# Opening of a sliding-window attention plus token/channel mixer kernel: loads, casts and score order of batch 0 rearranged

## The chip, the core and the metric

The kernel runs on one core of a Trainium2 chip. The core has five instruction streams that run on their own and meet through semaphores: TensorE (PE, matmuls; PEld is its weight load), VectorE (DVE), ScalarE (ACT), GpSimd (POOL) and SyncE (SP). Transfers between memory and the core run on 16 DMA engines; SP, ACT and POOL issue them. A transfer issued by POOL goes to the software queue (q0 in the profile), one issued by SP to q1, one issued by ACT to q10. The metric is the device time of one launch in microseconds (us), median over several runs.

## What is computed

For each of 8 batches: attention with 8 heads over 576 positions of 64 numbers, and then a mixer over positions and channels.

```python
scores = (1 / sqrt(64)) * q @ k.T                     # [8, 8, 576, 576]
rel = pos[:, None] - pos[None, :]
mask_plain = (rel >= 0) & (rel < 32)                  # heads 0 to 3
mask_dil = (rel >= 0) & (rel < 128) & (rel % 4 == 0)  # heads 4 to 7
attn = softmax(where(mask, scores, -1e9))
x = (attn @ v) with heads side by side                # [8, 576, 512]
h = relu(x.T @ w_tok1) @ w_tok2                       # mixes positions, 576 -> 256 -> 576
u = x + h.T
out = u + relu(u @ w_ch1) @ w_ch2                     # mixes channels, 512 -> 1536 -> 512
```

Inputs and the output are float32; matmuls run on float16 copies.

## The kernel before, in words

**Tiling.** A head has 576 positions: 512 "natural" ones and a tail of 64. Heads go in pairs, hp = 0 to 3; hp 0 and 1 have the plain window, hp 2 and 3 the dilated one. For the dilated heads only positions with the same remainder by 4 see each other, so the loads put positions m*4+r at partition m, column block r.

**Stages of a batch.** q and k are loaded in float32 (`load_qk`, tails of 64 by `load_tail`), cast to float16 (`cast_qk`, `cast_tails_qk`), turned by TensorE (`transposes`; tails of batch 0 by `first_tails`), and copied out of PSUM into `qz` and `kt`. `scores_plain` and `scores_dil` are generators of three steps for a pair of heads: one for each head's main blocks (tiles `sc`), and one for the small rest, the last block and the tail keys (tile `sm`). Each step ends with ScalarE's exponentials into `attp`, `attd` and `attt`. In batches 0 and 1 the mask is put into PSUM by a matmul of the identity with `veil`, a tile made once from the constants. `values` multiplies a head by v (tile `av`); VectorE divides by the row sum into `xn`. Then the token mixer (`h1p`, `up`), transposes of u, and the channel mixer: 12 blocks `gp` with the weight w3 (channel weight `moe_w_ch1`, three tiles of 512 columns, loaded by `load_w3` with a cast from float32) and the outputs `yp` with w4.

**Order.** All streams are scheduled by hand: the order in which the code is written is the order on each engine. For batch 0 the opening is written out line by line (lines 837 to 971). From line 973 on, later batches are interleaved with the channel mixer of the batch before, by `interleave`, which sorts steps by written times.

**The opening.** The constants (identity, permutation, masks; 128 x 672 float16) come by a transfer that POOL issues first (line 840). `emit_fixed` fills fixed tiles with zeros or ones. SP loads q and ACT loads k: heads 0 and 1, heads 2 and 3, tails, heads 4 to 7. SP then loads v in eight transfers (`load_v`): four blocks `l_vn` for the plain heads, the tail `l_vt`, two halves `l_vd` for the dilated heads, and `l_vx`. Each of these eight waits until one of the eight loads ahead of it has landed, since eight semaphores are used in turn. `warm(9)` is nine matmuls on a zero tile `idle`, with nothing that uses their results; `warm(3)` stands between the first transposes and the first scores. `ts` is the list of batch 0's score steps: `ts[5*hp]` and `ts[5*hp+1]` turn q and k of a pair (`tp(hp)` does both), and `ts[5*hp+2]` to `ts[5*hp+4]` are its three score steps (`sc(hp)` does all). POOL casts most of q, k and v, and issues the weights' transfers between these casts; a transfer that POOL issues takes time on POOL itself. Heads 4 to 7 of `values` need the casts of both `l_vd` halves and of `l_vx` (into `vt`, `cast_vx`).

**Batch 1's loads.** They are held back by `gate`: POOL writes one element into batch 1's tail tile after the copies `w2p`, and SP's loads wait for that.

Of the kernel before, what the change touches and what calls it, by code (L numbers as in the profile page):

```python
# [16 lines left out]
S = 576  # L17
# [51 lines left out]
def kernel(  # L69
# [11 lines left out]
    nc = tc.nc  # L81
# [77 lines left out]
    def emit_fixed():  # L159
        nc.gpsimd.memset(idle, 0.0)  # L160
# [7 lines left out]
        nc.vector.memset(attt, 1.0)  # L168

    def emit_fixed_late():  # L170
        for i in range(2):
            nc.gpsimd.memset(vv[i][64:128, 4], 0.0)
            nc.gpsimd.memset(vv[i][:, :, :, 64:65], 1.0)
            nc.gpsimd.memset(vt[i][:, :, 64:65], 1.0)
            nc.gpsimd.memset(w1t[i], 0.0)
        nc.gpsimd.memset(w2a[:, :, S:640], 0.0)


    l32 = {}
# [657 lines left out]
    ctx.enter_context(tc.manual_schedule())  # L837


    nc.gpsimd.dma_start(out=const, in_=const_dram)  # L840
    emit_fixed()
    new_qk(0)
    load_qk(0, "q", 0, 2, nc.sync)
    load_qk(0, "k", 0, 2, nc.scalar)
    load_qk(0, "q", 2, 4, nc.sync)
    load_qk(0, "k", 2, 4, nc.scalar)
    load_tail(0, "q", nc.sync)
    load_tail(0, "k", nc.scalar)
    load_qk(0, "q", 4, 8, nc.sync)
    load_qk(0, "k", 4, 8, nc.scalar)  # L850
    spark = fixed("spark", [1, 1], FP32)
    nc.scalar.activation(out=spark, in_=idle[0:1, 0:1], func=AF.Exp)
    load_v(0)
# [5 lines left out]
        c = slice(512 * i, 512 * i + 512)  # L859
        nc.gpsimd.dma_start(out=w3[i], in_=moe_w_ch1[:, c].rearrange("(x p) c -> p x c", p=128))  # L860

    cast_qk(0, "q", 0, nc.scalar)
    cast_qk(0, "k", 0, nc.vector)
    nc.vector.tensor_scalar(out=veil, in0=const[:, 256:CW], scalar1=1.0, scalar2=60000.0,
                            op0=ALU.subtract, op1=ALU.mult)
    cast_qk(0, "q", 1, nc.gpsimd)
    emit_fixed_late()
    cast_tails_qk(0, nc.gpsimd)
    nc.gpsimd.dma_start(out=w1p, in_=moe_w_tok1[0:512, :].rearrange("(m r) j -> m r j", r=4))
    for hp in range(2, 4):  # L870
        cast_qk(0, "q", hp, nc.gpsimd)
    nc.gpsimd.dma_start(out=w1t[0][0:64], in_=moe_w_tok1[512:S, :])
    nc.gpsimd.tensor_copy(out=spread[:, 3:515:4], in_=ident)
    cast_qk(0, "k", 3, nc.gpsimd)
    for s in range(4):
        cast_vn(0, s, nc.gpsimd)
    nc.gpsimd.dma_start(out=w2a[:, :, 0:S], in_=moe_w_tok2.rearrange("(p j) t -> p j t", j=2))
    load_w3(0)
    cast_vd(0, 0, nc.gpsimd)
    cast_vd(0, 2, nc.gpsimd)  # L880
    load_w3(1)
    cast_vx(0, nc.gpsimd)
    nc.gpsimd.dma_start(out=w1t[1][64:128], in_=moe_w_tok1[512:S, :])
    for jb in range(2):
        nc.gpsimd.tensor_copy(
            out=w2p[jb], in_=w2[jb][:, 0:512].rearrange("p (m r) -> p r m", r=4))

    warm(9)
    ts = [st[2] for st in score_steps(0, 0.0, 1.0)]
    va = [st[2] for st in value_steps(0, 0.0, 1.0)]  # L890

# [20 lines left out]
    ts[3]()  # L912
    cast_qk(0, "k", 1, nc.vector)
    tp(1)
    first_tails()
    ts[7]()
    ts[8]()
    cast_qk(0, "k", 2, nc.vector)
    ts[10]()
    ts[4]()  # L920
    ts[9]()
    ts[11]()
    tp(3)
    cast_tail_v(0, nc.vector)
    sc(2)
    va[0]()
    va[1]()
    sc(3)
    va[2]()
    va[3]()  # L930
    natural_w1(0)
# [40 lines left out]

    new_qk(1)
    gate(l32[(1, "t")][0:1, 0, 0:1], w2p[1][0:1, 0, 0:1])
    for nm in ("q", "k"):
        load_tail(1, nm, nc.sync)
    for h0 in (0, 4):
# [95 lines left out]
```

## Time and profile before

| | |
|---|---|
| time, median of 3 runs | 288.24 us (288.08 to 288.31) |
| the profiled execution, its own time | 289.66 us |
| its span in the profile | 287.8 us |
| busy: PE, DVE, ACT, POOL | 276.8, 132.1, 134.0, 163.0 us |
| instructions | 6995 |
| DMA | 52.63 MB, mean 183 GB/s |
| granted TensorE clock, mean | 1.0 |

The profiled execution reads 1.4 us over the median of the runs; its span is 0.4 us under that median. Times below are counted from the span's start. In the timelines a row has the start, the duration, the engine, the line of the kernel, the operation, what it writes and reads, how many instructions the row merges, and in brackets how long the engine had been idle and what ended that. The start of a matmul is recorded and its end is modelled: a matmul's duration holds its drain, which overlaps with the next one. The share of DMA time can stand above 100% of 16 engines because transfers in flight overlap.

### The profile page before, as it was taken

What the parts mean: (1) busy time and instruction counts of PE and PEld (TensorE: products, weight loads), DVE (VectorE), ACT (ScalarE), POOL (GpSimd) and SP (SyncE); (2) the same over time, 40 slices, a digit from 0 to 9 for tenths busy, and PEclk for the clock granted to TensorE, in tenths of its full rate; (3) what the DMA queues carried; (4) which work ended last, traced back from release to release, by engine and by line L of the source; (5) the groups of instructions that cost most, each with busy time, mean ns of one, the idle gap of its engine ahead of it and who ended that gap; (6) DMA issues with size and microseconds to landing.
All of it is one profiled execution on the core that took longest, in us unless ns stands there. A gap on an engine that the chain in (4) does not pass through costs nothing.

```text
span 287.8 us, 6995 instructions
## 1 busy us (share of the span) xinstructions
PE 276.8 (96%) x2838; PEld 210.9 (73%) x2838; DVE 132.1 (46%) x278; ACT 134.0 (47%) x265; POOL 163.0 (57%) x221
## 2 busy tenths in 40 slices
PE   5879999999999999999999999999999999999995
PEld 2777676888766886698776976797766966886594
DVE  7747658446764236414640164416440274421022
ACT  2854673263543804574447615482546534225500
POOL 6961860478865799449970999279952930000000
PEclk9999999999999999999999999999999999999999
DMA  7999999993999998979888978299974210431023
GB/s 218 263 211 218 283 225 207 320 218 82 328 210 192 264 264 230 139 164 350 226 159 182 330 224 186 57 219 329 193 150 95 85 64 2 91 112 37 0 76 108
DMA packets 105551, 52.63 MB, mean 183 GB/s; under 512 B 73872, under 2 KB 104464, under 8 KB 105520
## 3 DMA queue, kind: packets, MB, share of 16 engines
q1 hardware_dynamic: 101280, 47.07, 67.0%
q0 software_dynamic: 2640, 3.94, 8.0%
q10 hardware_dynamic: 1600, 1.18, 1.4%
q8 instruction: 22, 0.36, 0.6%
q14 instruction: 9, 0.07, 0.1%
HBM read 37.07 MB, written 9.44 MB: 162 GB/s over the span
## 4 chain that ended last, share of the span: by engine, by line
PE 80%; DMA 8%; DVE 3%; POOL 3%; issue 2%; ACT 2%; ACTq 1%; SPq 0%; POOLq 0%; DVEq 0%
PE yp L787 29%; PE gp L768 24%; DMA l_vd<-in_v_dram 4%; PE h1p L627 4%; PE yp L807 3%; DMA l_k<-in_k_dram 3%; PE up L639 3%; PE sc L510 3%; PE gt L759 3%; DVE xn L112 1%; DMA kr<-c_k 1%; PE h1p L625 1%; PE av L608 1%; PE up L650 1%; PE av L603 1%
## 5 line engine op out<-in xcount | busy, mean ns | idle before, releaser
L787 PE MATMUL yp<-w,gt 128*128 128x256 f16 x756 | 87.1, 273 | 0.0
L787 PEld LDWEIGHTS <-gt 128*128 128x128 f16 x768 | 78.6, 106 | 6.5
L106 ACT ACTIVATE gt<-gp 128x512 f16<-128x512 f32 x69 | 41.2, 597 | 76.3 <-PE gp L768 76.0
L768 PE MATMUL gp<-utd,w 128*128 128x512 f16 x144 | 54.7, 380 | 0.0
L768 PE MATMUL gp<-utm,w 128*128 128x512 f16 x144 | 54.6, 379 | 0.0
L768 PEld LDWEIGHTS <-w 128*128 128x128 f16 x384 | 39.2, 114 | 20.3 <-issue 0.5
L797 DVE TENSOR_TENSOR o<-yp,u 128x512 f32<-128x512 f32 x31 | 21.4, 691 | 63.1 <-PE yp L787 58.5
L112 POOL TENSOR_TENSOR attp<-attp,const 128x1280 f16<-128x1280 f16 x12 | 31.4, 2616 | 27.5 <-ACT attp L534 27.4
L112 DVE TENSOR_TENSOR xn<-av,rec 128x320 f16<-128x320 f32 x64 | 31.4, 491 | 2.2
L112 POOL TENSOR_TENSOR attd<-attd,const 128x1024 f16<-128x1024 f16 x12 | 25.3, 2132 | 1.6 <-ACT attd L534 1.6
L768 PE MATMUL gp<-uT,w 128*128 128x512 f16 x96 | 25.8, 379 | 0.0
L108 DVE TENSOR_SCALAR gt<-gp 128x512 f16<-128x512 f32 x27 | 18.5, 686 | 13.6 <-PE gp L768 13.1
L645 DVE TENSOR_TENSOR u<-up,xn 128x512 f16<-128x512 f32 x26 | 17.9, 690 | 7.5 <-PE up L639 7.5
L534 ACT ACTIVATE attp<-sc 128x480 f16<-128x480 f32 (+1 forms) x36 | 16.1, 536 | 7.4 <-PE sc L510 7.4
L102 POOL CAST c_k<-l_k 128x512 f16<-128x512 f32 x29 | 18.0, 628 | 1.9 <-DMA l_k<-in_k_dram 1.7
L102 POOL CAST c_q<-l_q 128x512 f16<-128x512 f32 x27 | 16.8, 629 | 3.1 <-DMA l_q<-in_q_dram 3.1
L616 DVE RECIPROCAL rec<-av 128x5 f32<-128x5 f32 x64 | 12.2, 190 | 13.8 <-PE av L613 13.7
L106 ACT ACTIVATE h<-h1p 128x256 f16<-128x256 f32 x29 | 11.1, 384 | 14.5 <-PE h1p L627 14.1
L399 POOL COPY kt<-kr 128x512 f16<-128x512 f16 x10 | 10.7, 1075 | 9.0 <-DMA kr<-c_k 9.0
L697 ACT COPY utd<-utm 128x512 f16<-128x512 f16 x12 | 12.8, 1135 | 4.1 <-DMA utm<-u 4.1
L102 POOL CAST vv<-l_vn 128x256 f16<-128x256 f32 x32 | 12.0, 420 | 4.3 <-DMA l_vn<-in_v_dram 4.1
L112 POOL TENSOR_TENSOR attt<-attt,const 128x512 f16<-128x512 f16 x12 | 14.0, 1165 | 0.0
(147 smaller groups left out, 459.9 us busy)
## 6 DMA issues: line engine op xcount, KB each, us to landing
out_dram<-o SPq DMA_DIRECT2D x72, 128.0 KB, 3.1
l_q<-in_q_dram SPq DMA_DIRECT2D x15, 512.0 KB, 7.2
l_k<-in_k_dram SPq DMA_DIRECT2D x14, 512.0 KB, 7.1
l_vn<-in_v_dram SPq DMA_DIRECT2D x32, 128.0 KB, 6.6
l_vd<-in_v_dram SPq DMA_DIRECT2D x16, 256.0 KB, 4.6
w<-in_moe_w_ch_dram POOLq DMA_DIRECT2D x6, 512.0 KB, 7.6
lt<-in_q_dram SPq DMA_DIRECT2D x8, 128.0 KB, 4.6
l_vt<-in_v_dram SPq DMA_DIRECT2D x8, 128.0 KB, 4.9
```

Of the source, the lines that this page charges most:

```text
L102: eng.tensor_copy(out=out, in_=in_)
L106: nc.scalar.activation(out=out, in_=in_, func=AF.Relu)
L108: eng.tensor_scalar_max(out=out, in0=in_, scalar1=0.0)
L112: eng.tensor_tensor(out=out, in0=x, in1=y, op=ALU.mult)
L534: nc.scalar.activation(out=out, in_=in_, func=AF.Exp, scale=0.125)
L616: nc.vector.reciprocal(out=rec[:, :, 0], in_=av[:, :, 64])
L627: nc.tensor.matmul(out=p, lhsT=w[:, s, j], rhs=x[:, s, c], start=False, stop=(s == 3))
L645: nc.vector.tensor_tensor(out=u16(b, s), in0=blocks4(p), in1=blocks4(xn[b][:, s]), op=ALU.add)
L697: nc.scalar.copy(out=natural(uTd[:, cb - 2]), in_=uTm[i][:, cb].rearrange("p r m -> p m r"))
L768: nc.tensor.matmul(out=p, lhsT=w3_block(cb, mb), rhs=uT[(b, cb)][0], start=(i == 0), stop=(i == 3))
L787: nc.tensor.matmul(out=p[:, c], lhsT=gta[:, mb, a0:m0 + 512:4] if half else gta[:, mb, a0:a0 + 128], rhs=w4[mb][:, c], start=(mb == 0), st ...
L797: nc.vector.tensor_tensor(out=blocks4(o32), in0=blocks4(p), in1=u16(b, s), op=ALU.add)
```

## The change

It touches the opening and, in four lines, the start of batch 1's loads.

- The constants are issued by SP, as its second transfer, instead of by POOL as its first.
- The loads of heads 4 to 7 of q and k go ahead of the tails.
- The first cast of q runs on VectorE instead of ScalarE. The fill of `attt` with ones runs on POOL instead of VectorE.
- POOL: the fills of batch 1's tiles (`emit_fixed_late(1)`) and the load of `w1t[1]` go behind the gate of batch 1's loads. The tails' cast goes behind the casts of q's and k's heads 4 to 7. The first third of w3 is issued behind both casts of `l_vd`, the second third behind the cast of `l_vx`.
- `warm(9)` becomes `warm(7)`.
- TensorE: the transposes and the main scores of hp 2 go ahead of the tails' transposes and of the small score steps of hp 0 and 1; the first main score step of hp 3 goes ahead of the first values.

```diff
@@ emit_fixed
-        nc.vector.memset(attt, 1.0)
-    def emit_fixed_late():
-        for i in range(2):
-            nc.gpsimd.memset(vv[i][64:128, 4], 0.0)
-            ...
+        nc.gpsimd.memset(attt, 1.0)
+    def emit_fixed_late(i):
+        nc.gpsimd.memset(vv[i][64:128, 4], 0.0)
+        ...
@@ opening
-    nc.gpsimd.dma_start(out=const, in_=const_dram)
     emit_fixed()
     new_qk(0)
     load_qk(0, "q", 0, 2, nc.sync)
     load_qk(0, "k", 0, 2, nc.scalar)
+    nc.sync.dma_start(out=const, in_=const_dram)
+    load_qk(0, "k", 2, 4, nc.scalar)
     load_qk(0, "q", 2, 4, nc.sync)
-    load_qk(0, "k", 2, 4, nc.scalar)
+    load_qk(0, "k", 4, 8, nc.scalar)
+    load_qk(0, "q", 4, 8, nc.sync)
+    load_tail(0, "k", nc.scalar)
     load_tail(0, "q", nc.sync)
-    load_tail(0, "k", nc.scalar)
-    load_qk(0, "q", 4, 8, nc.sync)
-    load_qk(0, "k", 4, 8, nc.scalar)
...
-    cast_qk(0, "q", 0, nc.scalar)
+    cast_qk(0, "q", 0, nc.vector)
     cast_qk(0, "k", 0, nc.vector)
...
     cast_qk(0, "q", 1, nc.gpsimd)
-    emit_fixed_late()
-    cast_tails_qk(0, nc.gpsimd)
+    emit_fixed_late(0)
     nc.gpsimd.dma_start(out=w1p, ...)
     for hp in range(2, 4):
         cast_qk(0, "q", hp, nc.gpsimd)
     nc.gpsimd.dma_start(out=w1t[0][0:64], in_=moe_w_tok1[512:S, :])
+    cast_qk(0, "k", 3, nc.gpsimd)
+    cast_tails_qk(0, nc.gpsimd)
     nc.gpsimd.tensor_copy(out=spread[:, 3:515:4], in_=ident)
-    cast_qk(0, "k", 3, nc.gpsimd)
     for s in range(4):
         cast_vn(0, s, nc.gpsimd)
     nc.gpsimd.dma_start(out=w2a[:, :, 0:S], ...)
-    load_w3(0)
     cast_vd(0, 0, nc.gpsimd)
     cast_vd(0, 2, nc.gpsimd)
+    load_w3(0)
+    cast_vx(0, nc.gpsimd)
     load_w3(1)
-    cast_vx(0, nc.gpsimd)
-    nc.gpsimd.dma_start(out=w1t[1][64:128], in_=moe_w_tok1[512:S, :])
...
-    warm(9)
+    warm(7)
@@ scores of batch 0
     tp(1)
-    first_tails()
     ts[7]()
     ts[8]()
     cast_qk(0, "k", 2, nc.vector)
-    ts[10]()
+    tp(2)
+    ts[12]()
+    ts[13]()
+    tp(3)
+    first_tails()
     ts[4]()
     ts[9]()
-    ts[11]()
-    tp(3)
+    ts[17]()
+    ts[14]()
     cast_tail_v(0, nc.vector)
-    sc(2)
     va[0]()
     va[1]()
-    sc(3)
+    ts[18]()
+    ts[19]()
     va[2]()
@@ batch 1
     gate(l32[(1, "t")][0:1, 0, 0:1], w2p[1][0:1, 0, 0:1])
+    emit_fixed_late(1)
+    nc.gpsimd.dma_start(out=w1t[1][64:128], in_=moe_w_tok1[512:S, :])
     for nm in ("q", "k"):
         load_tail(1, nm, nc.sync)
```

Two places show how instructions move. The first is VectorE in the opening, from the first casts to the first values. `tp_q` and `tp_k` are the transposed q and k, `tp_t` the transposed tails; `qz` and `kt` are the tiles that the scores read; `l_vt` is v's tail. Before:

```order
L168 MEMSET attt 128x2560
L102 CAST c_k_136<-l_k_0_109 128x512
...
L417 COPY qz<-tp_t 64x4x64 x2
L418 COPY kt<-tp_t 128x4x64
L102 CAST c_k_136<-l_k_1_110 128x512
L102 COPY qz<-tp_q_2_252 64x512 x2
L314 COPY kt<-tp_k_2_289 128x512
L314 COPY kt<-tp_k_3_302 128x512
L102 CAST vv_69<-l_vt_125 64x8x64
```

Now:

```order
L102 CAST c_q_134<-l_q_0_106 128x512
L102 CAST c_k_136<-l_k_0_108 128x512
...
L102 CAST c_k_136<-l_k_1_109 128x512
L102 COPY qz<-tp_q_2_237 64x512 x2
L314 COPY kt<-tp_k_2_244 128x512
L314 COPY kt<-tp_k_3_277 128x512
L417 COPY qz<-tp_t 64x4x64 x2
L418 COPY kt<-tp_t 128x4x64
L102 CAST vv_69<-l_vt_125 64x8x64
```

The fill of `attt` has left, a cast of q has come, and the tails' three copies now stand behind the copies of pairs 2 and 3.

The second is POOL from the casts of `l_vn` to the first casts of batch 1. `w_0` and `w_1` are thirds of w3, `w_81` is the weight `moe_w_tok2`, and the cast of one element into `lt` is the gate. Before:

```order
L102 CAST vv_69<-l_vn_122 128x4x64 x4
L877 DMA w_81<-in_moe_w_tok_dram 128x2x576
L860 DMA w_0_84<-in_moe_w_ch_dram 128x4x512
L102 CAST vv_69<-l_vd_123 128x4x2x64 x2
L860 DMA w_1_85<-in_moe_w_ch_dram 128x4x512
L102 CAST vt_71<-l_vx_124 128x4x64
L883 DMA w1t_80<-in_moe_w_tok_dram 64x256
L885 COPY w2p_82<-w_81 128x512
L885 COPY w2p_83<-w_81 128x512
L856 CAST lt_589<-w2p_83 1x1
```

Now:

```order
L102 CAST vv_69<-l_vn_122 128x4x64 x4
L877 DMA w_81<-in_moe_w_tok_dram 128x2x576
L102 CAST vv_69<-l_vd_123 128x4x2x64 x2
L860 DMA w_0_84<-in_moe_w_ch_dram 128x4x512
L102 CAST vt_71<-l_vx_124 128x4x64
L860 DMA w_1_85<-in_moe_w_ch_dram 128x4x512
L884 COPY w2p_82<-w_81 128x512
L884 COPY w2p_83<-w_81 128x512
L856 CAST lt_582<-w2p_83 1x1
L171 MEMSET vv_70 64x520
```

Each of the two weight transfers has gone one cast or two later; between the last `l_vd` cast and the `l_vx` cast there stands one such issue in both orders.

More of the change, by code (lines that the diff above doesn't have):

```diff
@@ L167, in emit_fixed @@
                 a.rearrange("p h (b c) -> p h b c", c=PST)[:, :, :, 128:PST], 0.0)
-        nc.vector.memset(attt, 1.0)
-    def emit_fixed_late():
-        for i in range(2):
-            nc.gpsimd.memset(vv[i][64:128, 4], 0.0)
[L173 to L176, printed above, removed]
+        nc.gpsimd.memset(attt, 1.0)
+    def emit_fixed_late(i):
+        nc.gpsimd.memset(vv[i][64:128, 4], 0.0)
+        nc.gpsimd.memset(vv[i][:, :, :, 64:65], 1.0)
+        nc.gpsimd.memset(vt[i][:, :, 64:65], 1.0)
+        nc.gpsimd.memset(w1t[i], 0.0)
+        if i == 0:
+            nc.gpsimd.memset(w2a[:, :, S:640], 0.0)
     l32 = {}
```

## The prediction

> **What bounds the kernel now.** I read the page first, then the busy time by stretch, then TensorE's timeline, and then what stands behind each of its waits.
>
> ```profile
> span 287.8 us, 6995 instructions
> core 0: us, PE busy (x) PEld busy (x) DVE busy (x) ACT busy (x) POOL busy (x), PEclk, DMA share, GB/s
> 0.00:6.79 6.79, 3.64 (x10) 1.29 (x11) 4.67 (x6) 1.99 (x3) 4.01 (x10) 1.00 0.71 214
> 6.79:20.85 14.06, 11.48 (x192) 9.98 (x191) 8.67 (x21) 10.40 (x22) 11.45 (x28) 1.00 1.19 247
> 60.00:280.00 220.00, 219.23 (x2182) 166.67 (x2181) 91.66 (x188) 103.58 (x202) 129.13 (x150) 1.00 0.70 170
> ```
>
> From 60 us on TensorE is busy for 219.23 of 220.00 us: nothing can be gained there by order. Up to 20.85 us it idles 2.58 us and does no useful work before 6.79 us (the 3.64 us there are the filler matmuls). So the change is worth what it takes off the moment at which TensorE passes the point of 20.85 us, as long as nothing behind that point holds it back.
>
> ```profile
> 2.54 3.63 PE L835 MATMUL idle_p<-idle 128*128 128x512 f16 x9 [2.54 <-POOL idle L160]
> 6.79 0.38 PE L309 MATMUL tp_q<-const,c_q 128*128 128x128 f16 x4 [0.61 <-DMA const<-consts]
> 7.23 0.81 PE L835 MATMUL idle_p<-idle 128*128 128x512 f16 x3
> ...
> 9.17 0.39 PE L309 MATMUL tp_k<-const,c_k 128*128 128x128 f16 x4
> 10.32 0.40 PE L411 MATMUL tp_t<-const,c_t 128*128 128x128 f16 x4 [0.77 <-POOL c_t L102]
> ...
> 15.69 0.19 PE L613 MATMUL av<-vv,attt 128*128 128x65 f16 x1 [0.42 <-DVE vv L102]
> ...
> 19.41 0.28 PE L608 MATMUL av<-vv,attd 128*128 128x65 f16 x4
> 20.85 0.19 PE L611 MATMUL av<-vt,attt 128*128 128x65 f16 x1 [1.16 <-POOL vt L102]
> ```
>
> The first transposes wait for the constants, the tails' transposes for their cast, the first values for v's tail, and at 20.85 us the dilated heads' values for POOL's cast `vt`. TensorE itself was done at 19.41 + 0.28 = 19.69 us. What made `vt` late:
>
> ```profile
> 11.76 7.27 DMA l_vd<-in_v_dram
> ...
> 14.60 0.72 POOL L877 DMA_DIRECT2D w<-in_moe_w_tok_dram  x1
> 15.31 0.77 POOL L860 DMA_DIRECT2D w<-in_moe_w_ch_dram  x1
> 19.08 0.63 POOL L102 CAST vv<-l_vd 128x512 f16<-128x512 f32 x1 [1.91 <-DMA l_vd<-in_v_dram]
> 19.65 0.74 POOL L860 DMA_DIRECT2D w<-in_moe_w_ch_dram  x1
> 20.38 0.42 POOL L102 CAST vt<-l_vx 128x256 f16<-128x256 f32 x1
> ```
>
> The second half of `l_vd` lands at 11.76 + 7.27 = 19.03 us; then a cast, the issue of a w3 third, and the cast of `l_vx`. So two paths meet at 20.85 us, v's being 1.2 us the longer, and both must get shorter.
>
> **Part 1: where TensorE starts.** Behind the constants.
>
> ```profile
> l_q<-in_q_dram SPq DMA_DIRECT2D x1, 256.0 KB, 3.4
> l_q<-in_q_dram SPq DMA_DIRECT2D x1, 256.0 KB, 5.2
> const<-consts POOLq DMA_DIRECT2D x1, 168.0 KB, 5.5
> 4.00 2.19 DVE L168 MEMSET attt<- 128x2560 f16 x1 [0.48 <-issue]
> 6.11 0.35 DVE L102 CAST c_k<-l_k 128x512 f16<-128x512 f32 x1
> 6.50 0.61 POOL L102 CAST c_q<-l_q 128x512 f16<-128x512 f32 x1 [1.76 <-DMA l_q<-in_q_dram]
> ```
>
> SP's first load of q, issued at 0.73, lands 3.4 us later, at 4.1; its second, issued at 1.25, lands at 6.4 (5.2). The constants now stand between the two in the same queue, so they land between 4.1 and 6.4 us, where before they landed at about 6.7 (issued 1.22, 5.5). They are two thirds of the second load's size and pass the point that it passed at the start; I take 5.5. The casts don't delay this: without the fill (4.00, 2.19 us) VectorE is free before 4, and two casts at 0.35 each behind q's landing at 4.1 and k's soon after are done by 5.0. The start moves by 6.79 - 5.5 = 1.3 us (bounds 0.4 and, by the casts, 1.8). The fill costs POOL something like VectorE's 2.19 us before its first cast at 6.50; POOL idles 1.76 us there and is relieved of issuing the constants, so this is hidden; a fill half as long again would put off pair 1's first cast by some 0.5 us, still ahead of its use.
>
> [...]
>
> **Part 2: TensorE from its start to the values of the dilated heads.** The work is the 11.48 us of the second stretch. The waits in it are new ones. Gone are 0.77 for the tails' cast and 0.42 for v's tail. What now holds TensorE are the copies out of PSUM:
>
> ```profile
> 8.80 1.03 ACT L461 ACTIVATE attp<-sc 128x480 f16<-128x480 f32 x2 [0.41 <-PE sc L425]
> 9.72 1.18 ACT L100 COPY qz<-tp_q 64x512 f16<-64x512 f16 x2
> 7.43 0.69 DVE L314 COPY kt<-tp_k 128x512 f16<-128x512 f16 x1 [0.20 <-PE tp_k L309]
> 10.76 0.61 DVE L417 COPY qz<-tp_t 64x256 f16<-64x256 f16 x2 [0.47 <-PE tp_t L411]
> 11.40 0.29 DVE L418 COPY kt<-tp_t 128x256 f16<-128x256 f16 x1
> 12.13 0.85 DVE L102 COPY qz<-tp_q 64x512 f16<-64x512 f16 x2
> ```
>
> - Scores of pair 1 need ScalarE's two copies of `qz`, which stand behind two exponentials. Before they ended 10.90 - 6.79 = 4.1 us after the first transposes, the first one 3.5. TensorE is through pair 1's transposes at 9.56 - 6.79 = 2.8. Idle 0.7 + 0.1 = 0.8 us; the removed 0.77 us lay in this same gap, so removing it gives nothing here.
> - Scores of pair 2 need `qz` (0.85) and then `kt` (0.69) from VectorE, right behind the transposes; the small scores that covered these copies before now come later. Idle about 0.85 + 0.69 less what the second transposes cover: 1.4 us.
> - The small scores need `kt` of pair 3 (0.69), the tails' `qz` (0.61) and `kt` (0.29), all on VectorE: 1.6 us less the 0.45 us of tails' transposes and first small scores: 1.15 us.
>
> Waits 3.4 us in place of 1.4 (12.90 us from 6.79 to 19.69 less 11.48). This supposes that q and k of heads 4 to 7 are there in time, by 10 us.
>
> ```profile
> 2.54 9.19 DMA l_k<-in_k_dram
> DMA packets 1224, 0.93 MB, mean 310 GB/s; under 512 B 408, under 2 KB 1224, under 8 KB 1224
> ```
>
> The second row is the stretch from 6.75 to 9.75 us. k's heads 4 to 7 landed at 2.54 + 9.19 = 11.73, with 256 KB of tails ahead; at 310 GB/s these are 0.85 us, and tails in short packets cost more, so the landing moves to 9.5 to 10.9. That holds even at the late end with 0.4 us lost.
>
> Sum: 5.5 + 11.5 + 3.4 = 20.4 us, where 19.69 stood before: TensorE's own path gets longer by 0.7 us, in spite of the earlier start, and is below the old 20.85 by 0.45 only.
>
> **Part 3: v's path.** POOL still issues one third of w3 (0.77) between the last `l_vd` cast and the `l_vx` cast, so the order alone gains nothing after the landing; what counts is when `l_vd` lands. In the stretch from 16.5 to 18.0 us:
>
> ```profile
> q1 hardware_dynamic: 109, 0.03, 9.4%
> q8 instruction: 1, 0.02, 4.3%
> ```
>
> SP's queue moved its last 0.03 MB there, yet the landing came at 19.03: some last pieces lagged, beside the 16 KB fetch of TensorE's instructions and POOL's `w` of 14.60 us. The fetch belongs to TensorE's place in its program, here around the first scores of pair 3, which it now reaches 1 to 1.5 us later; I take it to miss `l_vd`, and the landing at 17.1 us, just behind the bulk. Bounds 16.9 and 19.03. Then 17.1 + 0.6 + 0.75 + 0.45 = 18.9 us for `vt`: below TensorE's 20.4. If it stays at 19.03, `vt` stays at 20.85.
>
> So TensorE passes at 20.3 in place of 20.85 (the last drain overlaps): a gain of 0.55 us.
>
> **Part 4: what comes behind.** w3's first third is issued at 17.7 in place of 15.31, its second at 18.9 in place of 19.65.
>
> ```profile
> w<-in_moe_w_ch_dram POOLq DMA_DIRECT2D x1, 512.0 KB, 6.9
> q0 software_dynamic: 350, 0.35, 110.8%
> 28.80 0.62 POOL L102 CAST c_t<-lt 128x512 f16<-128x512 f32 x1 [6.05 <-PE tpu L673]
> 32.22 0.62 POOL L102 CAST c_q<-l_q 128x512 f16<-128x512 f32 x1
> 33.15 0.39 PE L309 MATMUL tp_q<-const,c_q 128*128 128x128 f16 x4
> ```
>
> The first row is the second third's time to landing (19.65 + 6.9 = 26.55), the second the queue's 0.35 MB in the 1.9 us from 19.1, so 512 KB take 2.8 us. Two of them behind a start at 17.7 + 2.0 end at 25.3, and 26.2 with the last pieces: 0.3 us earlier than now. Batch 1's loads come behind that, and TensorE needs them: it transposes pair 1's q at 33.15, cast done at 32.84, a margin of 0.3 us. So TensorE can gain 0.3 + 0.3 = 0.6 us before this holds it; 0.55 passes. The other edits lie under cover: the fills and the small weight of batch 1 in POOL's 6.05 us of idle before 28.80, and the channel mixer of batch 0, which follows the transposes of u that this row names, needs a third that lands by 24; without this cover the fills would cost their own length, about 1.5 us.
>
> **Sum:** 0.55 us off the profiled execution's 287.8 us of span (289.66 by its own clock). On the median of 288.24 us, which stands between the two: 288.24 - 0.55 = 287.7 us. A measurement of this kernel tells about 0.2%, 0.58 us, from no change.
>
> **The rivals.**
>
> *The waits are smaller and the loads run ahead.* If VectorE's two waits cost half (1.3 us in place of 2.55) and w3 ends 0.6 us earlier, TensorE passes at 19.1, and batch 1's loads then limit the gain to about 0.9: 287.3. For it: the copies may start as soon as each transpose ends; against: their sum is fixed by rows.
>
> *w3 goes behind v, and batch 1 waits for it (slower).* Place: the cast of pair 1's q in batch 1. If `l_vd` again lands at 19.03, nothing is gained at 20.85, the first third is issued at 19.7, two thirds end at 19.7 + 2.0 + 5.6 = 27.3 in place of 25.5, and after the margin of 0.3 TensorE loses 1.4 us: 289.6. It decides from a landing of 17.6 us on; at 18.2 it costs 0.6: 288.8. For it: both thirds now follow v in a stretch with the DMA engines full (share 1.19), where before the first ran beside `l_vd`'s last pieces. Against: the fetch is expected later.
>
> *The constants don't come earlier.* They are now behind 256 KB of q. At 6.4 us the sum of part 2 is 21.3: 0.45 us lost, 288.7; at 5.9, 287.9 to 288.2.
>
> *TensorE starts slow.* The nine fillers started 0.40 us apart and the three later ones 0.22. With seven, started 0.7 us earlier, they are done 0.7 us before the first transposes; if the switch is missed, eight transposes, three fillers and twelve score matmuls run at half speed: up to 1.8 us, of which 1.3 remain: 289.5. [...]
>
> **How the numbers follow.** Forecast 0.42 (287.4 to 288.0, so partly below 287.66); the better rival 0.23; w3 behind v 0.16; late constants 0.11; slow start 0.08. Faster by over 0.2%: 0.20 + 0.23 = 0.43. Within 0.2%: 0.22 + some 0.09 of the late constants and w3's mild end = 0.31. Slower: 0.26. The forecast's own range is 287.4 to 288.0; to hold eight in ten it must reach to the better rival's 287.1 and into the slower ones: 287.0 to 288.9.
>
> **What would show it.** Right: first transposes at 5.0 to 6.0; idle of 1 us or more before pair 2's scores and before the small scores, released by VectorE; `l_vd` landed by 17.6; values of the dilated heads with no wait for `vt`, at 20.0 to 20.6; batch 1's transposes of pair 1's q without a wait. Wrong: a wait for POOL's c_q around 33 us (w3 behind v), first transposes after 6.3, fillers still 0.4 us apart behind the first transposes, or the values before 19.5.

## The result and the profile after

The changed kernel takes 289.97 us (median of 6 runs, 289.26 to 291.62) against 288.27 us (288.08 to 288.52, 6 runs): a ratio of 1.0066, 95% interval [1.0037, 1.0094]. It is slower by 1.7 us, where 287.7 us was forecast. In a second measurement the ratio was 1.0081 [1.0052, 1.0110]. The profiled execution of the changed kernel took 289.26 us by its own time, with a span of 287.4; it is the fastest of the six.

TensorE's timeline of the changed kernel (start, length, engine, line, operation, count; in brackets the idle time ahead and what ended it):

```profile
1.31 3.17 PE L835 MATMUL idle_p<-idle 128*128 128x512 f16 x7 [1.31 <-POOL idle L160]
6.01 0.40 PE L309 MATMUL tp_q<-const,c_q 128*128 128x128 f16 x4 [1.53 <-DVE c_q L102]
6.58 0.81 PE L835 MATMUL idle_p<-idle 128*128 128x512 f16 x3
...
9.69 0.24 PE L425 MATMUL sc<-qz,kt 128*128 128x160 f16 x1 [0.69 <-DVE kt L314]
...
11.10 0.40 PE L309 MATMUL tp_q<-const,c_q 128*128 128x128 f16 x4 [0.30 <-POOL c_q L102]
...
13.17 0.24 PE L425 MATMUL sc<-qz,kt 128*128 128x128 f16 x1 [1.40 <-DVE kt L314]
...
15.62 0.19 PE L425 MATMUL sm<-qz,kt 128*128 128x64 f16 x1 [0.49 <-DVE qz L417]
...
16.27 0.20 PE L425 MATMUL sm<-qz,kt 128*128 128x64 f16 x1 [0.43 <-DVE kt L418]
...
21.32 0.19 PE L611 MATMUL av<-vt,attt 128*128 128x65 f16 x1
```

The dilated heads' values start without a wait for `vt`, as forecast, but at 21.32 instead of 20.3 us. Busy time from the first transposes to there (the second number is the length, the third what TensorE was busy):

```profile
6.01:21.32 15.31, 11.91 (x191) 10.06 (x192) 9.06 (x22) 9.89 (x21) 12.15 (x26) 1.00 1.14 223
```

TensorE thus starts 0.51 us later than forecast, is busy for 11.91 us instead of 11.5, and idles 15.31 - 11.91 = 3.40 us. The chain of waits of the same execution tells from where that moment is set:

```profile
2.22 8.16 DMA l_q<-in_q_dram
...
10.44 0.61 POOL c_q L102
...
11.10 0.41 PE tp_q L309 x4
...
11.53 0.42 DVE qz L102
...
11.96 0.43 DVE qz L102
...
12.42 0.70 DVE kt L314
...
13.17 0.24 PE sc L425
```

The start of TensorE is not in it. It begins with the load of q's heads 4 to 7, which lands at 2.22 + 8.16 = 10.38 us, and goes through POOL's cast, pair 2's transposes and three VectorE copies, end to end, beside which TensorE idles for 1.40 us. From the landing on, 10.94 us pass to 21.32.

The first cast of q, now on VectorE, took five times the 0.35 us that it was priced at, beside POOL's fill (rows of the timelines of VectorE and of POOL):

```profile
4.18 1.78 DVE L102 CAST c_q<-l_q 128x512 f16<-128x512 f32 x1 [0.67 <-DMA l_q<-in_q_dram]
...
3.44 2.24 POOL L168 MEMSET attt<- 128x2560 f16 x1
```

What was the kernel before doing in its usual runs? It was profiled twice more, and neither execution has the wait of 1.16 us for `vt` on which the forecast was built. The second one's timeline (span 285.8 us):

```profile
2.54 4.02 PE L835 MATMUL idle_p<-idle 128*128 128x512 f16 x9 [2.54 <-POOL idle L160]
...
7.37 1.23 PE L835 MATMUL idle_p<-idle 128*128 128x512 f16 x3
...
10.16 0.40 PE L411 MATMUL tp_t<-const,c_t 128*128 128x128 f16 x4 [0.28 <-POOL c_t L102]
...
19.21 0.19 PE L611 MATMUL av<-vt,attt 128*128 128x65 f16 x1
```

The values start at 19.21 us here, and at 19.98 in the other execution. So the change moved this point from 19.2 to 20.0 us up to 21.3, not from 20.85 down.

### The profile page after: what moved, and what is told of

It is laid out like the page before. It is cut to its first block, busy times and chain, and to the rows that moved or that the text cites. A ratio compares the mean times of both kernels' runs of the same rounds, so it can differ in the third digit from the quotient of the medians.

```text
span 287.4 us, 6986 instructions
## 1 busy us (share of the span) xinstructions
PE 276.4 (96%) x2836; PEld 210.6 (73%) x2836; DVE 131.8 (46%) x278; ACT 133.6 (46%) x264; POOL 164.7 (57%) x221
## 4 chain that ended last, share of the span: by engine, by line
PE 88%; DVE 5%; DMA 3%; ACT 1%; issue 1%; SPq 0%; POOL 0%; DVEq 0%
PE yp L787 29%; PE gp L768 27%; PE h1p L627 4%; PE up L639 4%; PE yp L807 4%; PE gt L759 3%; PE sc L510 3%; DMA l_q<-in_q_dram 3%; DVE xn L112 2%; PE h1p L625 1%; PE av L603 1%; PE av L608 1%; PE up L650 1%; PE sc L425 1%; PE sc L423 1%; PE av L601 1%
## 5 line engine op out<-in xcount | busy, mean ns | idle before, releaser
L768 PEld LDWEIGHTS <-w 128*128 128x128 f16 x384 | 39.2, 114 | 20.3 <-issue 0.5
```

Source lines behind the costliest of these rows:

```text
L768: nc.tensor.matmul(out=p, lhsT=w3_block(cb, mb), rhs=uT[(b, cb)][0], start=(i == 0), stop=(i == 3))
```

## The experiments

All were timed against the kernel before on the same chip; the ratio to it is given with its 95% interval. Two unchanged copies of the kernel before came out at 1.0015 [0.9997, 1.0033] and 0.9992 [0.9976, 1.0008], which is what no change looks like: a ratio of 1.0015 by itself says nothing. The theories at the outset: **the order** (TensorE's own path is longer, and `vt` was no limit); **the clock** (TensorE stays at or falls back to half speed, differently from launch to launch); **w3** (its thirds behind v make batch 1 late); **the opening** (constants, cast and fill).

### The two kernels again

> The kernel before, unchanged, for a second profile. The prediction rested on an execution that read 289.66 us where the timed runs read 288.1 to 288.5. Theory A (that execution had an unlucky landing of l_vd, and the timed runs do not wait for vt at 20.85): this profile shows l_vd landed by 17.6 us, the dilated heads' values at 19.5 to 19.9 with no wait for POOL's vt, and a span of 286.2 to 286.8. Rival B (the wait for vt is always there): values of the dilated heads at 20.7 to 21.0 behind a wait of 1.0 to 1.3 us, and a span of 287.5 to 288. Time 288.3 by both.

288.82 us (287.74 to 290.26, 12 runs). The first theory holds in its main point, there is no wait for `vt`; its span of 286.2 to 286.8 us was missed, for this execution (the slowest of the twelve) has 288.4. It lost its time in batch 1 instead: POOL's cast of batch 1's tails, which stands ahead of the cast that TensorE waits for, began at 29.99 us, when k's tails had landed, against 27.30 in the other copy. The second third of w3 was late too, 10.5 us after its issue at 17.81.

```profile
19.98 0.19 PE L611 MATMUL av<-vt,attt 128*128 128x65 f16 x1
...
32.10 0.40 PE L309 MATMUL tp_q<-const,c_q 128*128 128x128 f16 x4 [1.02 <-POOL c_q L102]
```

> The kernel before, unchanged, for another profiled execution. If the wait of 1.16 us for vt at 20.85 us belongs to one execution and not to the kernel, it is missing here too, the dilated heads' values start at 19.6 to 20.1 us, and the span is near 286.5 us (the timed runs' median less 1.86 us). If it is the kernel's, it stands here again at 1 us or more.

288.00 us (287.60 to 288.77, 8 runs), span of the profiled one 285.8: no wait for `vt`, as the first case says, and the values still earlier than it says (19.21); its rows stand above.

> The changed kernel, unchanged, for a second profile and more times. Its six times spread from 289.26 to 291.62, and the profiled one was the shortest. Theory A (what spreads is how late w3 and batch 1's loads come behind l_vd): opening as in the first profile, dilated heads' values at 21.3, and where the time is over 289.6 a wait for POOL's c_q or c_k around 33 us. Rival B (TensorE's clock comes late in some launches): fillers at 0.40 us apart behind the first transposes, and the values of the dilated heads 0.5 us or more later than 21.3. Time 289.3 to 291.6.

290.35 us (289.57 to 292.19, 8 runs), ratio 1.0081. In the profiled one of these (span 288.1) the fillers behind the first transposes ran at half speed, 1.49 us for three where the execution above took 0.81, and the values came 0.65 us later, as rival B says. By the trace's record of the granted clock TensorE came to full speed at 9.28 us here (the score matmuls start 0.13 us apart ahead of it and 0.07 us apart behind it) and at 4.47 us in the execution above:

```profile
6.85 1.49 PE L835 MATMUL idle_p<-idle 128*128 128x512 f16 x3
...
21.97 0.19 PE L611 MATMUL av<-vt,attt 128*128 128x65 f16 x1
```

### One part undone

The order alone undone (loads, place of the tails' cast and TensorE's order as before; constants, cast, fill and w3 as changed):

```diff
-    load_qk(0, "k", 4, 8, nc.scalar)
-    load_qk(0, "q", 4, 8, nc.sync)
     load_tail(0, "k", nc.scalar)
     load_tail(0, "q", nc.sync)
+    load_qk(0, "q", 4, 8, nc.sync)
+    load_qk(0, "k", 4, 8, nc.scalar)
...
     tp(1)
+    first_tails()
...
-    cast_qk(0, "k", 3, nc.gpsimd)
-    cast_tails_qk(0, nc.gpsimd)
```

> The changed kernel with one part undone: tails loaded ahead of heads 4 to 7, the tails' cast early on POOL, and TensorE's order of scores as before. Constants by SP, casts on VectorE, w3 behind v stay. Theory A (the late tails cost TensorE 1.3 us or more of waits for VectorE's copies): dilated heads' values at 19.5 to 20.0, no idle over 0.5 us before pair 2's scores, time 288.2 to 288.6. Rival B (the order is neutral, the loss is w3 behind v): values near 21, time 289.5 to 290.2.

289.30 us (288.25 to 290.16, 12 runs), 1.0031 [1.0013, 1.0049]: more than half of the loss is gone with the order, and some 0.9 us are left. It lies between the two cases. The profiled execution (290.09 us, among the slowest) was at half speed from 11.96 to 15.37 us (a granted clock of 0.58 from 12 to 16 us) and starts the values at 20.95.

The fill of `attt` off POOL's opening (four VectorE fills in gaps):

```diff
-        nc.gpsimd.memset(attt, 1.0)
...
     cast_qk(0, "k", 1, nc.vector)
+    nc.vector.memset(attt[:, 0], 1.0)
```

> The changed kernel, with the fill of attt taken off POOL's opening and put on VectorE in four pieces of 0.55 us, in gaps where it waits. Theory A (VectorE's cast of q took 1.78 us in place of 0.35 because POOL's 2.24 us fill ran beside it): the cast takes 0.35 us, the first transposes start at 5.0 to 5.2 instead of 6.01, and TensorE passes the dilated heads' values 0.5 to 0.9 us earlier; time 289.0 to 289.5. Rival B (the cast is long because its load was not all there): 1.78 us again, start at 6.0, time 289.9.

291.45 us (290.07 to 291.97, 6 runs), 1.0100 [1.0073, 1.0127], the slowest of all, although VectorE's cast is short and TensorE starts 1 us earlier:

```profile
4.20 0.43 DVE L102 CAST c_q<-l_q 128x512 f16<-128x512 f32 x1 [0.69 <-DMA l_q<-in_q_dram]
...
5.00 0.59 PE L308 MATMUL tp_q<-const,c_q 128*128 128x128 f16 x4 [0.52 <-DVE c_k L102]
...
11.33 0.40 PE L308 MATMUL tp_q<-const,c_q 128*128 128x128 f16 x4 [1.31 <-POOL c_q L102]
```

The earlier start is given back in full at pair 2, where TensorE now waits 1.31 us for the cast of q's heads 4 to 7 instead of 0.30. And the clock falls (the mean granted clock is 0.986 to 0.994 in all six runs), which the busy time by stretch shows in its third column from the end (the granted clock):

```profile
12.00:16.00 4.00, 2.60 (x26) 2.60 (x26) 1.90 (x4) 1.37 (x3) 3.43 (x9) 0.58 1.19 239
16.00:19.50 3.50, 3.05 (x37) 2.78 (x35) 1.80 (x5) 2.02 (x6) 2.76 (x6) 0.51 0.94 167
```

w3 alone undone (its thirds where the kernel before issues them):

```diff
+    load_w3(0)
     cast_vd(0, 0, nc.gpsimd)
     cast_vd(0, 2, nc.gpsimd)
-    load_w3(0)
-    cast_vx(0, nc.gpsimd)
     load_w3(1)
+    cast_vx(0, nc.gpsimd)
```

> The changed kernel with w3's first two thirds issued where the kernel before has them (the first ahead of l_vd's casts, the second ahead of l_vx's); all else as changed. If w3 behind v costs its 1.2 us in the whole change too, the median falls from 290.35 to 289.2 us. If that cost is hidden, because TensorE reaches batch 1 later than w3 and batch 1's loads, the median stays within 0.4 us of 290.35, though w3's second third lands by 26.6 us and the DMA engines no longer move under 110 GB/s between 18 and 20 us.

290.29 us (289.22 to 292.16, 9 runs), 1.0064 [1.0040, 1.0089]: w3's price is hidden in the whole change. The values start at 21.31 us, to 0.01 us where they did with w3 behind v.

Order and w3 both undone, so that constants, cast, fill and the seven fillers are left:

> The changed kernel with everything of the order undone (loads, tails' cast, TensorE's order) and w3 where the kernel before has it: what is left is the constants by SyncE's queue, the first cast of q on VectorE, attt's fill on POOL and seven fillers. If this opening costs nothing, the median is at 288.0 to 288.5 us, and the 1 us that the run with only the order undone lost to the kernel before was w3's. If the opening itself loses (the cast stretched to 1.7 us beside the fill, the clock at half speed), the median is at 289.0 us or more.

288.83 us (287.61 to 289.75, 12 runs), 1.0011 [0.9994, 1.0028]: the opening by itself costs nothing that can be told, and brings nothing. It starts at 6.02 us and is at the values when the first of the two unchanged copies is (19.98), partly at half speed (1.49 us for the three fillers):

```profile
6.02 0.61 PE L309 MATMUL tp_q<-const,c_q 128*128 128x128 f16 x4 [1.53 <-DVE c_q L102]
...
6.84 1.49 PE L835 MATMUL idle_p<-idle 128*128 128x512 f16 x3
...
19.99 0.19 PE L611 MATMUL av<-vt,attt 128*128 128x65 f16 x1
```

### One part alone, on the kernel before

The order alone (the diff of the first run of "One part undone", reversed, in the kernel before):

> The kernel before with one part of the change: heads 4 to 7 loaded ahead of the tails, the tails' cast behind k's, and TensorE's order with the tails' transposes behind pair 3's. If the new order is the loss, the waits for VectorE's copies of 1.4 us and some 0.9 us stand in its profile, the dilated heads' values start 1 to 1.5 us later than in the kernel before's profile (19.98 us), and the median is 0.8 to 1.5 us above the kernel before. If the order is harmless and the loss lies elsewhere (constants, fill, w3), the median is within 0.5 us of the kernel before.

290.28 us (290.07 to 291.25, 6 runs), 1.0079 [1.0058, 1.0100]: the whole loss, from this part. TensorE's timeline:

```profile
10.27 0.24 PE L425 MATMUL sc<-qz,kt 128*128 128x160 f16 x1 [0.69 <-DVE kt L314]
...
12.09 0.40 PE L309 MATMUL tp_k<-const,c_k 128*128 128x128 f16 x4 [0.49 <-DVE c_k L102]
...
13.57 0.25 PE L425 MATMUL sc<-qz,kt 128*128 128x128 f16 x1 [1.03 <-DVE kt L314]
...
16.02 0.19 PE L425 MATMUL sm<-qz,kt 128*128 128x64 f16 x1 [0.49 <-DVE qz L417]
...
16.67 0.20 PE L425 MATMUL sm<-qz,kt 128*128 128x64 f16 x1 [0.43 <-DVE kt L418]
```

These are nearly the same waits, 3.13 us in sum, with the first transposes at 6.71 and the values at 21.73 us. Only the second has another cause: VectorE's cast of k held the chain for 1.82 us, from 10.21 to 12.03, while POOL was busy for all of 9.50 to 12.00 us. Some 0.25 us of the loss stands in no timeline: the runs' own times lie 2.07 to 2.16 us over their spans here, 1.8 to 1.9 us in the unchanged copies.

The constants alone (by SyncE's queue behind q's first load, all else as before):

> The kernel before with the constants' load alone moved to SyncE's queue, behind the first load of q. The first casts and the fill stay where they were. If the constants are what holds the start, the first transposes start at 5.5 to 6.2 us in place of 6.8 to 7.0. If the opening's gain reaches the end, the median is 0.5 to 0.8 us below the kernel before; if batch 1's loads hold it (a wait of 1 us for POOL's c_q stood at 32.10 us in the kernel before's second profile), nothing or at most 0.2 us is gained, and the wait at 32 us grows by as much as the start gained.

289.77 us (288.27 to 290.65, 11 runs), 1.0048 [1.0030, 1.0066]: against both cases. TensorE starts at 5.24 us, then waits 0.67 us for k's first cast, which stands behind VectorE's fill; the three fillers then take 1.49 us, and the values start at 19.82, which is 0.61 us behind the unchanged second copy. In batch 1 the lag grows to 1.65 us (the third transposes at 33.16 instead of 31.51): POOL's cast of the tails begins at 29.15, when k's tails have landed, instead of 27.30. Whether the constants' new place delays that landing stays open, since it also differed between the two unchanged copies. With the changed kernel's other opening edits this loss is not there (1.0011).

w3 alone behind v, with batch 1's fills and small weight later:

> The kernel before with the other part: w3's first two thirds issued behind v's casts, batch 1's memsets and small weight later. If w3 behind v makes batch 1 late, its second third lands at 28.3 us or later, the wait for POOL's c_q at 32 us is 1 us or more, and the median is 0.3 to 1.4 us above the kernel before. If it is hidden, the median is within 0.3 us of the kernel before and w3 lands no later than 28.3 us.

289.27 us (288.29 to 290.49, 12 runs), 1.0034 [1.0017, 1.0050]: about 1 us, without the order to hide it. Of this run, and then of the unchanged second copy, the stretch from 18 to 20 us (the last two columns are the share and the GB/s of the DMA engines) and the second third's issue:

```profile
18.00:20.00 2.00, 2.00 (x34) 1.84 (x31) 1.11 (x4) 0.98 (x3) 1.29 (x4) 1.00 0.48 44
...
19.14 0.74 POOL L860 DMA_DIRECT2D w<-in_moe_w_ch_dram  x1
```

```profile
18.00:20.00 2.00, 2.00 (x37) 1.84 (x35) 0.99 (x3) 1.17 (x2) 1.08 (x4) 1.00 1.17 177
...
17.30 0.75 POOL L860 DMA_DIRECT2D w<-in_moe_w_ch_dram  x1
```

With w3 behind v's casts the DMA engines stand half idle between v's last bytes and w3's first ones: (177 - 44) GB/s over 2 us are 0.27 MB that have to be moved later. That this delays batch 1 fits what follows: k's tails land late, POOL's cast of the tails begins at 28.87 us instead of 27.30, and batch 1's transposes wait 0.15, 0.19 and 0.16 us in a row at 30.86 to 32.93. The lag behind the unchanged second copy is 0.39 us at the values (19.60) and 1.42 us at the last of these.

### The clock and the cast

Eleven fillers in place of seven in the changed kernel (`warm(11)`):

> The changed kernel with eleven fillers instead of seven ahead of the first transposes (warm(11)), so that TensorE has no idle 1.5 us between 4.48 and 6.01 us. If the idle stretch is what lets TensorE's clock stay at half speed in some launches, the fillers behind the first transposes are 0.21 us apart in the profile, the spread of the timed runs shrinks from 2.6 us to under 1.5 us, and the median falls by 0.5 to 1 us below the changed kernel's 290.35 us. If the loss lies in the order of the work alone, the median stays at 289.7 to 290.4 us and the values of the dilated heads at 21.3 us or later.

290.57 us (289.26 to 291.44, 6 runs), 1.0078 [1.0051, 1.0104]: no gain. The idle before the first transposes is filled, but the profiled execution fell to half speed at 12.37 us, amid the waits for the copies:

```profile
12.00:16.00 4.00, 2.75 (x26) 2.75 (x27) 1.22 (x4) 1.52 (x3) 3.70 (x9) 0.55 1.19 241
16.00:19.50 3.50, 3.05 (x42) 2.78 (x40) 1.73 (x5) 2.02 (x6) 2.69 (x5) 0.54 0.95 168
```

Fillers in those waits as well:

```diff
-    warm(7)
+    warm(11)
...
     tp(1)
+    warm(3)
...
     tp(2)
+    warm(6)
...
     first_tails()
+    warm(3)
```

> The changed kernel with filler matmuls in its idle stretches: eleven ahead of the first transposes, and three, six and three more where TensorE waits for copies (before pair 1's scores, before pair 2's scores, behind the tails' transposes). The fillers change no wait, they only keep TensorE busy. If the spread of the changed kernel's times and part of its loss come from a clock that falls back to half speed behind idle stretches, no half-speed stretch stands between 6 and 280 us in the profile, the runs lie within 1 us of each other, and the median falls from 290.4 to 289.0 to 289.5 us. If the clock is no cause, the median stays at 290.2 to 290.8 us.

289.48 us, 1.0044 [1.0029, 1.0059]; nine of ten runs lie between 289.35 and 289.82, the tenth at 291.06. The profiled one has no half-speed stretch, and the values start to the hundredth where they did in the changed kernel's own profile:

```profile
9.50:12.00 2.50, 2.12 (x24) 1.43 (x23) 0.92 (x4) 1.82 (x4) 1.56 (x3) 1.00 1.41 196
12.00:16.00 4.00, 3.73 (x43) 2.58 (x41) 2.34 (x6) 2.12 (x4) 3.63 (x9) 1.00 1.16 251
...
21.32 0.19 PE L611 MATMUL av<-vt,attt 128*128 128x65 f16 x1
```

So these fillers are worth 0.6 to 1.1 us of the changed kernel's median (1.0066 and 1.0081 to 1.0044, in different sessions and with intervals that meet) and, but for one run, its spread; the 1.3 us that are left fit the path. That it is all the clock's doing is not shown. Of the changed kernel's fourteen timed runs only two, the slowest of the second measurement, have a mean granted clock below 1.0 (0.994 and 0.982); the six of the first all have 1.0 and still spread by 2.4 us. A slow start could be part of that, but the record can't tell: it reads 1.00 also while the fillers above took 1.49 us.

The opening of the last run of "one part undone", with eleven fillers in place of seven:

> The run with constants and fill alone (the change without its order and with w3 where it was), with eleven fillers instead of seven, so that TensorE is not idle for 1.5 us before its first transposes. If that run's times (287.61 to 289.75 us) are spread by a clock that comes late in some launches, the profile has no half-speed stretch behind 6 us, the spread shrinks, and the median falls to 287.7 to 288.1 us, faster than both kernels. If batch 1's loads or the tails' cast hold it, the median stays within 0.3 us of that run's 288.83 us.

288.57 us (287.92 to 289.54, 12 runs), 1.0008 [0.9993, 1.0023]: the second case. TensorE is early and waits, for casts whose loads have only just landed:

```profile
10.10 0.40 PE L411 MATMUL tp_t<-const,c_t 128*128 128x128 f16 x4 [0.98 <-POOL c_t L102]
...
12.33 0.40 PE L309 MATMUL tp_q<-const,c_q 128*128 128x128 f16 x4 [1.00 <-POOL c_q L102]
...
19.91 0.19 PE L611 MATMUL av<-vt,attt 128*128 128x65 f16 x1
```

The constants' 168 KB now stand ahead of q's tails in SyncE's queue. From 1.7 to 2.6 us, this run and then the unchanged second copy, with the time from issue to landing at the end (issues at 2.22 and at 1.75 us):

```profile
lt<-in_q_dram SPq DMA_DIRECT2D x1, 128.0 KB, 7.1
```

```profile
lt<-in_q_dram SPq DMA_DIRECT2D x1, 128.0 KB, 5.7
```

q's tails land at 2.22 + 7.1 = 9.3 instead of 7.5 us. Before, k's tails, landing at 8.8, were the later ones of the pair; now q's are, 0.5 us later. The cast of both begins at 9.43 us, the moment that it had before (9.49), though batch 1's fills no longer stand ahead of it on POOL: the constants' load came sooner here, that of q's tails 1.8 us later.

POOL's fill of `attt` in four pieces, with nine fillers:

```diff
-        nc.gpsimd.memset(attt, 1.0)
+        for i in range(4):
+            nc.gpsimd.memset(attt[:, i], 1.0)
```

> As the run with constants and fill alone, but POOL's fill of attt is four fills of a quarter each, and nine fillers stand ahead of the first transposes. If VectorE's first cast is held by one long POOL fill until that ends, it takes 0.4 to 1.0 us instead of 1.7 and the first transposes start at 5.2 to 5.6 us. If the two merely share a rate, the cast still takes 1.5 us or more. Where the start is earlier, the tails' landing at 9 us holds TensorE all the same, so I expect the median at 288.0 to 288.8 us.

288.97 us (287.91 to 290.42, 12 runs), 1.0013 [0.9998, 1.0029]. The cast takes 0.71 us:

```profile
4.22 0.71 DVE L102 CAST c_q<-l_q 128x512 f16<-128x512 f32 x1 [0.71 <-DMA l_q<-in_q_dram]
...
3.44 2.90 POOL L169 MEMSET attt<- 128x640 f16 x4
```

The 1.5 us or more of a shared rate did not come. With one long fill the cast ends at 4.18 + 1.78 = 5.96, 0.28 us behind that fill's end (3.44 + 2.24 = 5.68), and in the run before this one 0.27 us behind (5.96 for 5.69); here it ends at 4.93, amid the four pieces, which run on to 3.44 + 2.90 = 6.34. The pieces take 2.90 us where the one fill took 2.24, and the cast of k that follows beside them takes 0.93 us where it took 0.41 behind the long fill. The first transposes started at 5.27, and nothing came of it: TensorE then waited 1.79 us for the tails' cast, and the profiled execution, the slowest of the twelve, was at half speed from 11.62 to 18.45 us (its mean granted clock is 0.987, and four transposes took 0.61 to 0.63 us instead of 0.40).

### Towards a faster version

Three edits of the kernel before, from what the profiles pointed to. Batch 1's gate and loads ahead of w3's second third:

> The kernel before with one move: the gate that lets SyncE issue batch 1's loads stands ahead of w3's second third, so that these loads start at 18 us instead of 21.3. In the profiles the DMA engines move only 100 to 200 GB/s between 18 and 24 us. If batch 1's loads are what holds TensorE at 32 us, pair 1's q of batch 1 lands by 30 us, the waits at 31 to 34 us go, and the median falls by 0.3 to 0.8 us. If it is hidden, the median moves by less than 0.2 us; if w3's second third is delayed past its use at 32 us, it rises by 0.5 us or more.

288.54 us (287.44 to 289.21, 12 runs), 1.0001 [0.9985, 1.0018]. The loads were issued from 17.56 us on instead of 21.35, and q landed at 28.9 us, no sooner than in the unchanged second copy (28.5): it took 9.9 us from its issue instead of 5.8.

Batch 1's fills behind w2p's copies, so that the tails' cast comes sooner:

> The kernel before with one part of the change: batch 1's memsets and small weight later on POOL (here behind w2p's copies), so that the tails' cast is no longer behind them. If POOL's c_t is what TensorE waits for in the kernel before (0.3 to 0.8 us at 10.2 us), the cast ends at 9.6 instead of 10.2 us, and the dilated heads' values start up to 0.5 us sooner; the median then falls by 0.2 to 0.5 us if batch 1's loads allow it, and stays within 0.2 us if they don't.

288.88 us (288.37 to 289.70, 12 runs), 1.0015 [1.0002, 1.0029], no more than an unchanged copy showed. The cast came 0.25 us sooner (9.24 for 9.49), TensorE waited for q's heads 4 to 7 in its place (0.63 us at 12.13), and batch 1's loads, gated behind the moved fills, were issued 1.95 us later.

Both together with the constants by SyncE's queue and VectorE's fill in four pieces behind the casts:

> A version meant to be faster than both: the kernel before with its order, the constants by SyncE's queue as in the change, VectorE's fill of attt in four pieces behind the casts (so that k's first cast is not behind it), batch 1's fixed fills and small weight later, and batch 1's loads let go ahead of w3's second third. If start and batch 1's loads together are the limit, the first transposes start by 5.3 us, k's follow without a wait, the dilated heads' values start by 18.9 us, no wait for POOL's c_q stands at 31 us, and the median is 0.8 to 1.5 us below the kernel before. If the loads keep holding batch 1, it is within 0.3 us of it.

289.40 us (288.40 to 290.65, 12 runs), 1.0026 [1.0009, 1.0042]. TensorE waited 2.29 us for the tails' cast at 10.79 and fell to half speed behind it (a mean granted clock of 0.994; four transposes took 0.61 to 0.63 us from 15.04 on); the values start at 21.82 us. No version was faster than the kernel before.

## Why the prediction was wrong

**The step that failed first: the base.** "So two paths meet at 20.85 us, v's being 1.2 us the longer" was true of one execution. It took 289.66 us by its own time with a span of 287.8, that is 1.86 us beside the span; the median of 288.24 thus belongs to a span of 286.4, and the profiled execution was 1.4 us slower than the usual one. The 1.16 us for `vt` were most of that, and are absent from both further profiles. (One of these was slower still, by batch 1; so the wait was one cause of a slow execution among others.) The forecast named the two numbers, put the median "between the two", and took 0.55 us off a wait that the median doesn't hold. Without that wait the old order's own path, 19.69 us in the forecast's own working and 19.21 to 19.98 as measured, was the base, and the forecast's own 20.4 would have said slower. On top of that, its 20.4 fell 0.9 us short of the 21.32 measured: 0.51 in the start (part 1 below) and 0.4 in the work, 11.91 for 11.5 us. From 19.2 or 20.0 up to 21.3 us is a loss of 1.3 to 2.1 us, which covers the measured 1.7. The two further profiles of the kernel before have 11.9 and 12.0 us of work up to the values too; the 11.48 was the lowest of three.

**Part 2: waits right, chain wrong.** The terms: 0.8 measured as 0.69 (VectorE's `kt`, not ScalarE's `qz`, came last), 1.4 as 1.40, 1.15 as 0.49 + 0.43 = 0.92, in sum 3.01 for 3.35. The fifth wait, 0.30 for q's heads 4 to 7, was named but stands in no term; that all five make 3.31, so near the forecast's 3.4, is partly luck. And they were added to a start. The chain of waits shows that, once TensorE is early enough, the sum runs from the landing of q's heads 4 to 7 at 10.38 us. The forecast allowed "0.4 us lost" there; the run that starts at 5.00 us lost 1.31 at that place, so there the whole gain of the start went. For tails in short packets, which the forecast calls dearer, the first profile of the kernel before has 310 GB/s from 6.75 to 9.75 us with 408 of 1224 packets under 512 B, and 264 GB/s from 9.75 to 12 us with 1677 of 1853.

**Part 1: 5.5 us forecast, 6.01 measured.** The constants were not late: the runs with the constants in SyncE's queue have them at 5.0 to 5.2 us, so the rival that they come no earlier is out, though q's tails pay for it. The mis-sized term is "two casts at 0.35 each": the first took 1.78 beside the fill that the forecast called hidden on POOL, and 0.43 in the run with the fill off POOL. A fill that was covered on its own engine thus cost its neighbour 1.35 us.

**Part 3: right in its number, by luck.** `l_vd` landed at 16.9 and there is no wait for `vt`, but the change did not do that: in the two unchanged copies it landed at 17.2 and 16.7. Nor did the instruction fetch move out of the way, as the forecast supposed; it starts at 16.8 us (q8 in the profile) in the changed kernel, behind 106 matmuls, and at 16.9 in the kernel before, behind 154. So no run shows that this first fetch goes by TensorE's place in its program, from which the forecast had its landing at 17.1. The landing at 19.03 belonged to one execution, and why it was late is open.

**Part 4:** w3's second third was forecast to land at 26.2 us, 0.3 earlier; in the changed kernel it landed at 18.61 + 9.2 = 27.8. Alone the later issue costs about 1 us, most likely because the DMA engines idle ahead of it. In the whole change this is hidden by TensorE's lateness, as the run with w3 put back shows; so the rival "w3 goes behind v" was right on its mechanism and wrong on its place, and no wait stands at batch 1's q. The parts alone lose 1.4, 2.3 and 1.0 us (0.48, 0.79 and 0.34% of 288.2) and the whole 1.9 to 2.3 by its ratios. They don't add up; for the last two the likely reason is that they act on different paths, of which only the longer counts.

**The rival of the slow start** was seen in one of the changed kernel's two profiled executions, and cost 0.65 us at the values where 1.3 was forecast. It is not what the prediction missed: the other execution had full speed from 4.47 us on and was late all the same. A fall in the middle of the program is what the forecast did not look for: in the run with eleven fillers the clock fell amid waits of 0.69, 0.39 and 1.39 us, and the half-speed stretches shown in rows above lie within 12 to 19.5 us, with clocks of 0.51 to 0.58. What sets the moment of the rise or of the fall is not shown.

What stays open: why loads of the same kernel land so differently from one execution to the next (w3's second third 10.5 and 8.2 us after its issue, batch 1's k tails 7.4 and 5.1). A wait of 1.02 us in batch 1 stands behind such a landing in one unchanged copy, and none in the other. Open too is what spreads the changed kernel's runs at a granted clock of 1.0.

## What to carry to other kernels

Before a wait is priced, ask whether the timed runs contain it: look at the profiled execution's span, subtract from the median what lies between own time and span in runs of the same kernel, and if its span is longer than that, its most unusual wait is the first suspect. An order that consumes the latest load earlier moves the start of the chain to that landing, and earlier starts are worth nothing ahead of it. Independent work that stood in a wait for copies was not only cover; it went with a TensorE clock that stayed up (no timed run of the kernel before has a mean granted clock below 0.997, of the changed kernel's fourteen two have 0.994 and 0.982).

## What the runs showed of the hardware that was not expected

- A float32 to float16 cast of 128x512 on VectorE took 0.35 to 0.43 us in rows above without a POOL fill beside it, 1.78 and 1.82 us beside one POOL fill of 2.24 us (the changed kernel, and the opening with eleven fillers), and 0.71 us beside a fill in pieces of 128x640. Beside the one long fill it ended about 0.3 us behind the fill's end.
- TensorE's clock fell to half speed in the middle of the program, in the first two runs below with no gap over 1.4 us near it (granted clocks of 0.58 and 0.55 from 12 to 16 us). The last two rows below are alike, 1.77 of 2.50 us busy, and one kept full speed: the busy share of this stretch does not decide.

The stretch ahead, of the run with the fill off POOL, of the run with eleven fillers (both fell), and of the changed kernel (which did not):

```profile
9.50:12.00 2.50, 1.19 (x16) 0.81 (x13) 1.82 (x4) 1.03 (x2) 1.34 (x4) 1.00 1.41 189
```

```profile
9.50:12.00 2.50, 1.77 (x20) 1.27 (x20) 0.85 (x3) 1.81 (x4) 1.47 (x3) 1.00 1.41 180
```

```profile
9.50:12.00 2.50, 1.77 (x20) 1.26 (x20) 0.92 (x4) 1.82 (x4) 1.56 (x3) 1.00 1.41 203
```
